# Attention and two expert layers in one kernel: own bank for the Sinkhorn sums, later conversions, token sums from turned tiles, work moved from VectorE to POOL

## The chip, the cores and the metric

The kernel runs on one core of a Trainium2 chip, as one launch. The metric is device time in microseconds, from a run without a profiler; a profiled execution is taken beside it. Five engines work at once, each through its own queue in order: TensorE (PE, with PEld for its weight loads), VectorE (DVE), ScalarE (ACT), GpSimd (POOL) and SyncE (SP), which issues all the transfers.

## The reference

Three blocks follow each other on 1536 tokens (two sequences of 768) with 512 features:

```python
# 1. banded attention, 8 heads of 64: key j is kept for query i where
#    0 <= i - j < 96, or j < 8; linear distance bias per head; softmax; times v
# 2. eight experts, all of them on every token, weighted by a Sinkhorn matrix
logits = x @ w_gate
P = np.exp(logits - logits.max())
for _ in range(8):
    P /= P.sum(1, keepdims=True) + 1e-09
    P /= P.sum(0, keepdims=True) + 1e-09
    P *= N / E
for e in range(E):
    out += P[:, e:e+1] * (np.maximum(x @ w1[e], 0.0) @ w2[e])      # 512 -> 1024 -> 512
# 3. h = max(x @ w1, x @ w2, x @ w3); result h @ w_out              # 512 -> 768 -> 512
```

All of it is in float32.

## The kernel before

Every float32 operand is split into an upper part, rounded for TensorE (`...h`, a ScalarE copy), and a lower part, the rest (`...l`, a subtraction on VectorE or POOL); a product is three matmuls, upper by upper, upper by lower and lower by upper.

**Attention** (`near_attention`, L415) runs over 48 units of 256 queries and one head, with one step per unit. In a step each engine gets work of three units: the scores of the next one, the turning and the value product of this and of the last one, and the splits of the one after. `s_min` and `s_norm` (L520, L546) are the softmax; `split_qk` and `split_v` (L450, L476) split queries, keys and values, the lower parts of keys and values on POOL; `x_evac` (L332) adds up two heads, writes x to DRAM (`xd`) and splits it. `tables_rest` (L141) makes the distance tables that units from number 8 on use. Expert 0's weights come in eight tiles `w0` at the steps of `W0AT` (2, 4, 6, 8 to 12): `w0_hi` (L193) copies the upper part, and `w0_lo` (L199) subtracts the lower part on VectorE, one step later. Expert 0 and the gate's logits run on TensorE between the units' matmuls.

**The expert loop** starts when attention ends. Experts 1 to 7 go through `w1` by a Strassen-like scheme: a group is 7 products of 2 by 3 matmuls instead of 8. A list of hooks, fillers and jobs, all with step numbers that are written out by hand, sets the order: group G starts at step 7G, and `REL` says at which step of a group each of its products stands (1:0, 2:2, 6:4, 7:8, 5:10, 4:12, 3:13, so that three groups overlap). A step holds a product, the hooks of that step, and one filler, which is mostly a piece of the output product. There are four passes: p = 0 and 1 are the experts for either half of the tokens (28 groups each), p = 2 and 3 are the third block (9 groups each, `base[2]` is step 392, `base[3]` 455). In p = 2 and 3, no output piece stands between the products for long stretches.

The products of a group write into PSUM banks `b1` (three buffers), `b2` (two) and `b3` (one); `BANK` assigns products 5 and 3 to `b2`, product 2 to `b3`. `keep` (L1162) copies a bank on ScalarE, `add` (L1197) adds another to it on VectorE, `fin` (L1177) applies the relu or the maximum and splits. Loads go through five buffers `raw` in the order of their job steps; `feed` (L938) issues as many as there are free buffers.

**Sinkhorn** (L886 to L926) runs beside the first 25 steps. A round is a row step on VectorE (`sink_rows`), a matmul with ones for the column sums (`col`) into bank `b3`, and the column step on VectorE (`turn`). **Conversions** (L1090) turn the third block's weights, which come as 64-bit numbers, into float32 on VectorE, nine passes each, 24 conversions from step 15 on, 14 steps apart; `sums_m` (L1008) then makes sums of weight blocks on POOL.

**Token sums.** The scheme needs four sums of x blocks, t1 to t4, for every pass. `chain_at` (L1058) loads two blocks from DRAM, subtracts on POOL (L1069), stores the result to `xt[p]` (L1070), and loads it again for the next of the four. For p = 2 and 3 x is the output of the experts: `x2_tile` (L1077) turns a tile of it on TensorE, ScalarE copies it, and it is stored to DRAM (`x2d`), from where `chain_at` reads. `put` (L1038) loads and splits the blocks and the sums.

Of the kernel before, what the change touches and what calls it, by code (L numbers as in the profile page):

```python
# [24 lines left out]
def kernel(  # L25
# [40 lines left out]
    def load_first(i, t):  # L66
# [74 lines left out]
    def tables_rest():  # L141
# [24 lines left out]
    xt = [dpool.tile([4, 128, 2 * QT], F32, name=f"xt{p}") for p in range(4)]  # L166
# [26 lines left out]
    def w0_hi(j):  # L193
        o = 0
        for (h, l), n in zip(w0[j], W0N[j]):
            nc.scalar.copy(h[:, 0:n], w0raw[j][:, o : o + n])
            o += n

# [133 lines left out]
    def x_evac(op, pool, o, hp, n):  # L332
# [8 lines left out]
        def late():  # L341
# [3 lines left out]
            nc.vector.tensor_tensor(  # L345
# [15 lines left out]
    def chain(p, raw, done, cols=slice(None)):  # L361


        def one(o, a, b, nm, free):
            def go():
                ro = raw(o)
                nc.gpsimd.tensor_tensor(out=ro, in0=raw(a), in1=raw(b), op=ALU.subtract)
                nc.sync.dma_start(out=xt[p][XT.index(nm)][:, cols], in_=ro)
                for f in free:
                    done(f)  # L370

            return go

        return [
            one("b11", "b12", "b11", "t1", ()), one("b12", "b22", "b12", "t3", ("b12",)),
            one("b22", "b22", "b11", "t2", ("b11",)),
            one("b21", "b21", "b22", "t4", ("b22", "b21")),
        ]

    def chain0():  # L380

        fs = []
        for kk in range(2):
# [6 lines left out]
            c = slice(kk * QT, kk * QT + QT)  # L390
            fs += [load, None] + chain(0, rr.get, lambda nm: None, c)
# [23 lines left out]
    def near_attention():  # L415
        with ExitStack() as st:
# [179 lines left out]
            def s_x(u):  # L596
# [4 lines left out]
                return x_evac(opu.pop(u // 2), ap, tb * 256, h // 2, 256)  # L601
# [11 lines left out]
            tables_rest()  # L613
# [5 lines left out]
            for s in range(NU + 1):  # L619
# [33 lines left out]
                if s in W0AT:  # L653
                    wlate = W0AT.index(s)
                    w0_hi(wlate)
# [21 lines left out]
    def full_attention():  # L677
        with ExitStack() as st:
# [4 lines left out]
            ps_y = st.enter_context(tc.tile_pool(name="gps_y", bufs=1, space=PSUM))  # L683
            for j in range(8):
# [169 lines left out]
    pools = {"b1": ps_b1, "b2": ps_b2, "b3": ps_b3, "yp": ps_y}  # L854
# [57 lines left out]
    def sink_turn(n):  # L912
        box = {}

        def col():
            box["ps"] = bank("b3", "c")
# [21 lines left out]
    def feed():  # L938
        while job_q and flying["n"] < 5 and job_q[0][3] <= flying["slot"]:
# [4 lines left out]
            elif k2 == "t":  # L944
                nc.sync.dma_start(out=r[:, 0 : 2 * QT], in_=src)
            elif k2 == "c":
                nc.sync.dma_start(out=r.bitcast(I32), in_=src)
            else:
# [65 lines left out]
    for u in range(9):  # L1014
        s = 28 * u + 50
# [30 lines left out]

    for p in range(4):
        for nm, r in USE.items():
            t = nm in XT
            src = xt[p][XT.index(nm)] if t else x_block(xd if p < 2 else x2d, p, nm)  # L1050
            job(base[p] - 6 + r, ("x", p, nm), src, "t" if t else "x", (-9, 177, base[1] + 185, base[2] + 48)[p])
# [4 lines left out]
    SUM = (("t1", "b12", "b11"), ("t3", "b22", "b12"), ("t2", "b22", "t1"), ("t4", "b21", "t2"))  # L1056

    def chain_at(p, s, d, src):  # L1058
        for n, (o, a, b) in enumerate(SUM):
            for x in (a, b):  # L1060
                t = x in XT
                job(
                    s + n * d, ("c", p, n, x), xt[p][XT.index(x)] if t else x_block(src, p, x),
                    "t" if t else "x", s + n * d - (d - 1 if t and d < 8 else 8),
                )

            def go(n=n, o=o, a=a, b=b):
# [369 lines left out]
```

## Time and profile before

| | |
|---|---|
| median of 3 runs | 1373.66 us (1373.36 to 1376.17) |
| profiled execution | 1376.38 us, its span 1374.6 us |
| instructions | 19793 |
| mean granted TensorE clock | 0.98 of full speed |
| busy in the span | PE 1319.0 us (96%), PEld 1190.9 (87%), DVE 948.5 (69%), ACT 700.8 (51%), POOL 645.9 (47%) |
| moved by DMA | 171.26 MB, 125 GB/s |

A busy share is the mean over stretches with different limits. Matmuls are pipelined, so the durations of single ones overlap; the distance from one to the next is what counts.

### The profile page before, as it was taken

The numbers are of one execution on the slowest core, as the hardware profiler recorded it, in microseconds if no ns is written. First come the engines' busy times: TensorE is split into PE (matmuls) and PEld (weight loads), VectorE is DVE, ScalarE is ACT, GpSimd is POOL, SyncE is SP. The second block draws the span as 40 slices with busy tenths as digits, with TensorE's granted clock in tenths as the row PEclk, the third lists the DMA queues.
The fourth block names the chain that finished last, engine by engine and source line by source line (L and its number), as shares of the span: only waits on it lengthen the run. The fifth ranks groups of instructions, "written<-read, shape, count | busy, mean of one in ns | idle before, by whom it ended". The sixth has DMA issues, their size and how long they took to land.

```text
span 1374.6 us, 19793 instructions
## 1 busy us (share of the span) xinstructions
PE 1319.0 (96%) x6984; PEld 1190.9 (87%) x6984; DVE 948.5 (69%) x1507; ACT 700.8 (51%) x1415; POOL 645.9 (47%) x716
## 2 busy tenths in 40 slices
PE   5899999879999999999999999999999999979998
PEld 3789998768888898889888888898898889878987
DVE  7877786586776878787888677677876556455361
ACT  6777776444444444454554454544444445445351
POOL 5545663236445555545455443454444442273251
PEclk8799999889999999999999999999999999999999
DMA  5543540432233343333454343432324135466231
GB/s 156 165 127 89 161 150 18 143 122 93 85 116 111 125 138 126 123 127 108 132 179 142 108 129 104 149 128 90 129 77 132 65 118 184 129 242 215 102 104 46
DMA packets 67307, 171.26 MB, mean 125 GB/s; under 512 B 6784, under 2 KB 25984, under 8 KB 67200
## 3 DMA queue, kind: packets, MB, share of 16 engines
q1 hardware_dynamic: 67200, 169.91, 38.4%
q8 instruction: 57, 0.93, 0.3%
q14 instruction: 50, 0.41, 0.1%
HBM read 143.15 MB, written 26.74 MB: 124 GB/s over the span
## 4 chain that ended last, share of the span: by engine, by line
PE 88%; DVE 5%; ACT 2%; issue 2%; DMA 1%; POOL 1%; DVEq 0%; SPq 0%; POOLq 0%; ACTq 0%
PE yp L238 42%; PE b L1156 35%; PE hp L221 5%; PE o L593 2%; PE t L567 2%; PE s L507 1%; DVE sal L961 1%; POOL raw L1069 0%; PE lp L298 0%; DMA x2d<-x2t 0%; DMA raw<-xt 0%; ACT sbh L979 0%; PE x L1081 0%; DVE u L1204 0%; DMA raw<-w 0%
## 5 line engine op out<-in xcount | busy, mean ns | idle before, releaser
L238 PE MATMUL yp<-w2h,xl 128*128 128x512 f32 x744 | 295.4, 397 | 0.0
L238 PE MATMUL yp<-w2l,xh 128*128 128x512 f32 x744 | 293.9, 395 | 0.0
L238 PE MATMUL yp<-w2h,xh 128*128 128x512 f32 x744 | 290.3, 390 | 0.0
L154 POOL TENSOR_TENSOR xl<-u,xh 128x384 fp32r<-128x384 f32 x112 | 115.8, 1034 | 349.7 <-ACT xh L153 345.3
L974 POOL TENSOR_TENSOR raw<-raw 128x256 f32<-128x256 f32 x260 | 230.7, 888 | 74.1 <-DVE sbl L961 49.0
L238 PEld LDWEIGHTS yp<-w2h,xl 128*128 128x128 f32 x744 | 139.6, 188 | 29.7
L238 PEld LDWEIGHTS yp<-w2h,xh 128*128 128x128 f32 x744 | 140.0, 188 | 18.8 <-DVE y L1254 0.5
L238 PEld LDWEIGHTS yp<-w2l,xh 128*128 128x128 f32 x744 | 139.6, 188 | 18.3
L1254 DVE SCALAR_TENSOR_TENSOR y<-yp,pm,y 128x512 f32<-128x512 f32 x168 | 124.3, 740 | 15.5 <-PE yp L238 15.4
L1164 ACT COPY u<-b 128x384 f32<-128x384 f32 x148 | 70.2, 477 | 119.0 <-PE b L1156 105.3
L1184 ACT ACTIVATE s<-s 128x384 f32<-128x384 f32 x56 | 29.5, 526 | 194.9 <-DVE s L1204 194.9
L961 DVE TENSOR_TENSOR sbl<-raw,sbh 128x768 fp32r<-128x768 f32 x56 | 75.2, 1342 | 62.9 <-ACT sbh L979 61.4
L226 DVE SCALAR_TENSOR_TENSOR xl<-b,xh 128x384 fp32r<-128x384 f32 x56 | 31.1, 555 | 106.0 <-ACT xh L225 104.8
L961 DVE TENSOR_TENSOR sal<-raw,sah 128x1024 fp32r<-128x1024 f32 x68 | 84.6, 1244 | 25.6 <-ACT sah L990 25.5
L1204 DVE TENSOR_TENSOR u<-b,u 128x384 f32<-128x384 f32 x136 | 74.6, 549 | 39.1 <-PE b L1156 37.8
L961 DVE TENSOR_TENSOR w2l<-raw,w2h 128x1024 fp32r<-128x1024 f32 x62 | 83.0, 1338 | 13.2 <-ACT w2h L1026 13.2
L1164 ACT COPY s<-b 128x384 f32<-128x384 f32 x74 | 35.4, 478 | 105.9 <-PE b L1156 105.8
L154 POOL TENSOR_TENSOR xl<-s,xh 128x384 fp32r<-128x384 f32 x56 | 59.7, 1066 | 53.6 <-ACT xh L153 53.6
L990 ACT CAST sah<-raw 128x1024 fp32r<-128x1024 f32 x74 | 77.3, 1044 | 4.5 <-POOL raw L974 2.5
L1184 ACT ACTIVATE u<-u 128x384 f32<-128x384 f32 x112 | 59.1, 528 | 24.0 <-DVE u L1204 24.0
L462 POOL TENSOR_TENSOR k<-kqv,k 128x384 fp32r<-128x384 f32 (+1 forms) x46 | 47.2, 1026 | 48.2 <-ACT k L461 48.2
L979 ACT CAST sbh<-raw 128x768 fp32r<-128x768 f32 x74 | 61.5, 832 | 10.5 <-DMA raw<-w 6.0
(275 smaller groups left out, 3573.9 us busy)
## 6 DMA issues: line engine op xcount, KB each, us to landing
raw<-w SPq DMA_DIRECT2D x163, 512.0 KB, 3.7
kqv<-a SPq DMA_DIRECT2D x32, 416.0 KB, 3.2
raw<-w32s SPq DMA_DIRECT2D x18, 512.0 KB, 4.1
raw<-xt SPq DMA_DIRECT2D x22, 384.0 KB, 3.2
raw<-x2d SPq DMA_DIRECT2D x18, 384.0 KB, 3.9
w<-cb SPq DMA_DIRECT2D x24, 256.0 KB, 2.3
raw<-xd SPq DMA_DIRECT2D x12, 384.0 KB, 4.1
w32s<-raw SPq DMA_DIRECT2D x9, 512.0 KB, 2.6
```

The lines of the kernel that those rows point to most:

```text
L154: lo_eng.tensor_tensor(out=lo, in0=src, in1=hi.bitcast(F32), op=ALU.subtract)
L221: nc.tensor.matmul(ps, a[:, q], b, start=k == 0, stop=k == 11)
L238: nc.tensor.matmul(ps, a, b, start=kf == first and i == 0, stop=kf == last and i == 2)
L961: (eng or nc.vector).tensor_tensor(out=l, in0=src, in1=h.bitcast(F32), op=ALU.subtract)
L974: nc.gpsimd.tensor_tensor(out=b[o], in0=b[x], in1=b[z], op=op)
L979: nc.scalar.copy(h, r)
L990: nc.scalar.copy(h, jobs[key])
L1156: nc.tensor.matmul(s[BANK[m]], a[:, c], b[:, kk], start=k == 0 and m in FIRST, stop=k == 5 and m in LAST, skip_group_check=True,)
L1164: nc.scalar.copy(t, st[G]["b1"])
L1184: nc.scalar.activation(src, src, AF.Relu)
L1204: nc.vector.tensor_tensor(out=o, in0=s[b], in1=s[nm], op=ALU.add)
L1254: nc.vector.scalar_tensor_tensor(out=y[n], in0=ps, scalar=pm[:, n, e : e + 1], in1=y[n], op0=ALU.mult, op1=ALU.add)
```

## The change

- Attention: the gate's weights are made (POOL) at the end of step 0 instead of ahead of the loop; `tables_rest` moves from ahead of the loop to step 1, and its six copies from VectorE to POOL. The lower parts of the first four `w0` tiles are subtracted on POOL in parts of 256 columns, two per step, instead of on VectorE in one go. For the first 256 tokens, `x_evac`'s lower part is on POOL.
- PSUM: `b2` has one buffer instead of two; a new bank `c` takes the column sums of Sinkhorn and the turned tiles. The Sinkhorn start stands ahead of the first `s_sum`, and the rounds are at steps 2, 5, ... 23 instead of 1, 4, 7, 10, 13, 17, 20, 24.
- Conversions, `sums_m` and the token sums of pass 1 start 14 steps later.
- `xt[p]` is stored as eight blocks of 384 columns instead of four of 768. For p = 2 and 3 the sums are taken on POOL from two turned tiles in SBUF, 256 columns each, and stored once per pair.
- The output product of pass 2 (`o_piece`) is divided by features: twelve matmuls of the first two feature blocks per tile from step `base[3]` - 6 on, copied out by ScalarE, and six of the last block after `base[3]` + 8, added by VectorE; before it was nine and nine in one PSUM bank after `base[3]` + 8.

```diff
-    nc.gpsimd.memset(wg2.bitcast(F32)[:, :, 2 * E :], 0.0)
-    nc.gpsimd.tensor_copy(wg2[:, :, 0:E], wgr)
-    nc.gpsimd.tensor_tensor(
-        out=wg2[:, :, E : 2 * E], in0=wgr, in1=wg2[:, :, 0:E].bitcast(F32), op=ALU.subtract
-    )
+    def gate_weights():
+        nc.gpsimd.memset(wg2.bitcast(F32)[:, :, 2 * E :], 0.0)
...
-            nc.vector.tensor_copy(dst, src)
+            nc.gpsimd.tensor_copy(dst, src)
...
-    xt = [dpool.tile([4, 128, 2 * QT], F32, name=f"xt{p}") for p in range(4)]
+    xt = [dpool.tile([8, 128, QT], F32, name=f"xt{p}") for p in range(4)]
...
+    def w0_lo_parts(j):
+        def one(h, l, n, o, last):
+            def go():
+                c = slice(n, n + 256)
+                nc.gpsimd.tensor_tensor(
+                    out=l[:, c], in0=w0raw[j][:, o : o + 256], in1=h.bitcast(F32)[:, c],
+                    op=ALU.subtract,
+                )
...
-            nc.vector.tensor_tensor(
+            eng.tensor_tensor(
                 out=xvl[:, o // 256, hp, c], in0=tmp, in1=hi.bitcast(F32), op=ALU.subtract
             )
...
+                eng = nc.gpsimd if tb == 0 else nc.vector
...
-            tables_rest()
+            wparts = []
...
                 if s in W0AT:
-                    wlate = W0AT.index(s)
-                    w0_hi(wlate)
+                    j = W0AT.index(s)
+                    w0_hi(j)
+                    if j < 4:
+                        wparts += w0_lo_parts(j)
+                    else:
+                        wlate = j
+                for f in wparts[:2]:
+                    if f():
+                        consumed()
+                wparts = wparts[2:]
+                if s == 0:
+                    gate_weights()
+                if s == 1:
+                    tables_rest()
...
-    ps_b2 = ctx.enter_context(tc.tile_pool(name="ps_b2", bufs=2, space=PSUM))
+    ps_b2 = ctx.enter_context(tc.tile_pool(name="ps_b2", bufs=1, space=PSUM))
+    ps_c = ctx.enter_context(tc.tile_pool(name="ps_c", bufs=1, space=PSUM))
...
-            box["ps"] = bank("b3", "c")
+            box["ps"] = bank("c", "c")
...
-        s = 28 * u + 50
+        s = 28 * u + 64
...
+    C1 = {o: 106 + 28 * n for n, (o, _, _) in enumerate(SUM)}
+    P2 = [base[1] + 50 + 28 * i for i in range(3)]
+    P3 = [base[2] + 21 + 4 * i for i in range(3)]
...
+            ready = (-9, C1[nm] + 1 if t else -9, P2[2] + 6, P3[2] + 6)[p]
...
+    def x2_sums(p, i):
+        t = i if p == 2 else 6 + i
+        a, b = x2t.pop(t), x2t.pop(t + 3)
+        r = jobs["x2", p, i]
+        t1, t2, t3, t4 = [r[:, 256 * n : 256 * n + 256] for n in range(4)]
+        lo, hi = slice(0, 256), slice(256, 512)
+        for o, x, z in (
+            (t1, b[:, lo], a[:, lo]), (t2, b[:, hi], t1), (t3, b[:, hi], b[:, lo]),
+            (t4, a[:, hi], t2),
+        ):
+            nc.gpsimd.tensor_tensor(out=o, in0=x, in1=z, op=ALU.subtract)
+        nc.sync.dma_start(
+            out=xt[p][:, :, 128 * i : 128 * (i + 1)].rearrange("a p n -> p a n"),
+            in_=r.rearrange("p (a n) -> p a n", a=8),
+        )
+        done(("x2", p, i))
+
+    for p, ss, d in ((2, P2, 2), (3, P3, 1)):
+        for i, s in enumerate(ss):
+            t = i if p == 2 else 6 + i
+            job(s + d, ("x2", p, i), None, None, s - 8)
+            at(s, lambda t=t: x2_tile(t))
+            at(s + d, lambda t=t: x2_tile(t + 3))
+            at(s + 2 * d, lambda p=p, i=i: x2_sums(p, i))
...
-    for t in range(6):
-        fillers.append((base[2] + 20 + t, lambda s, t=t: x2_tile(6 + t, "yp")))
-    for t in range(6):
-        fillers.append((base[3] + 8, o_piece(2, t, (0, 3, 1), True, False)))
-        fillers.append((base[3] + 8, o_piece(2, t, (4, 2, 5), False, True)))
+    for i, t in [(i, t) for i in range(2) for t in range(6)]:
+        s = base[3] + (8 + t if i else 2 * t - 6)
+        fillers.append((s, o_piece(2, t, ((0, 3, 1, 4), (2, 5))[i], i == 0, i == 1, True)))
...
-        convert(n // 2, n % 2, 14 * n + 15)
-    chain_at(1, 92, 28, xd)
-    for t in range(6):
-        at(base[1] + 43 + 7 * t, lambda t=t: x2_tile(t, "b2"))
-    chain_at(2, 288, 28, x2d)
-    chain_at(3, base[2] + 36, 4, x2d)
-
-    for n, c in enumerate((1, 4, 7, 10, 13, 17, 20, 24)):
+        convert(n // 2, n % 2, 14 * n + 29)
+
+    for n, c in enumerate(range(2, 24, 3)):
...
-        2: (lambda: s_sum(0), sink_start, lambda: s_add(1)),
+        2: (sink_start, lambda: s_sum(0), lambda: s_add(1)),
```

## Rows read from the trace of the kernel before

**Rows 1.** Busy time by stretch: PE, PEld, DVE, ACT, POOL, clock, DMA share, GB/s.
```profile
12.00:56.00 44.00, 34.14 (x148) 27.05 (x149) 36.71 (x107) 33.08 (x100) 23.97 (x42) 0.69 0.52 151
...
256.00:311.00 55.00, 41.60 (x194) 37.15 (x194) 41.94 (x96) 25.89 (x45) 20.18 (x23) 0.86 0.35 113
311.00:1184.00 873.00, 873.00 (x4355) 783.65 (x4355) 627.45 (x775) 420.73 (x729) 423.17 (x429) 1.00 0.37 120
1184.00:1257.00 73.00, 62.49 (x346) 59.10 (x345) 42.19 (x53) 33.38 (x59) 36.94 (x22) 0.95 0.64 211
```

**Rows 2.** Chain that ended last, attention stretch: start us, us, what.
```profile
12.61 1.13 DVE db L150 x3
...
23.89 1.64 DVE w_0l L202
...
40.61 1.91 DVE w_2l L202
```

**Rows 3.** Timeline of POOL and DVE in attention: start us, us, instruction.
```profile
8.24 0.50 POOL L486 TENSOR_TENSOR vhl<-y,vhl 128x128 fp32r<-128x128 f32 x1
...
19.32 0.74 POOL L462 TENSOR_TENSOR k<-kqv,k 128x256 fp32r<-128x256 f32 x1
...
42.45 0.15 DVE L550 TENSOR_SCALAR am<-am 128x2 f32<-128x2 f32 x1
...
44.47 1.19 POOL L462 TENSOR_TENSOR k<-kqv,k 128x384 fp32r<-128x384 f32 x1
...
44.83 0.86 DVE L550 TENSOR_SCALAR am<-am 128x2 f32<-128x2 f32 x1
```

**Rows 4.** Chain that ended last, expert loop.
```profile
262.42 2.29 PE b L1156 x6
...
310.60 0.23 PE c L917 x2
310.83 2.16 PE yp L238 x6
...
1184.44 2.09 PE b L1156 x12
1186.52 0.44 PE x L1081 x4
...
1192.11 6.35 DMA x2d<-x2t
...
1228.57 3.87 DMA raw<-w
...
1349.14 21.82 PE yp L238 x96
```

**Rows 5.** Timeline of DVE at the start of the expert loop.
```profile
254.28 0.68 DVE L226 SCALAR_TENSOR_TENSOR xl<-hp,xh 128x512 fp32r<-128x512 f32 x1
...
262.20 0.17 DVE L920 TENSOR_SCALAR cs<-c 128x8 f32<-128x8 f32 x1
...
263.98 0.33 DVE L893 TENSOR_REDUCE cs<-pm 128x8 f32<-128x96 f32 x1
```

**Rows 6.** The page's costliest groups, whole span: busy, mean ns | idle before, releaser.
```profile
L974 POOL TENSOR_TENSOR raw<-raw 128x256 f32<-128x256 f32 x260 | 230.7, 888 | 74.1 <-DVE sbl L961 49.0
...
L961 DVE TENSOR_TENSOR sal<-raw,sah 128x1024 fp32r<-128x1024 f32 x68 | 84.6, 1244 | 25.6 <-ACT sah L990 25.5
...
L979 ACT CAST sbh<-raw 128x768 fp32r<-128x768 f32 x74 | 61.5, 832 | 10.5 <-DMA raw<-w 6.0
```

**Rows 7.** Timeline of PE and DVE after 1184: product 5 and the add.
```profile
1216.18 0.54 DVE L1204 TENSOR_TENSOR u<-b,u 128x384 f32<-128x384 f32 x1
...
1217.13 0.33 PE L1156 MATMUL b<-t1h,sah 128*128 128x384 f32 x1
...
1225.52 0.33 PE L1156 MATMUL b<-t1h,sah 128*128 128x384 f32 x1
...
1227.80 0.54 DVE L1204 TENSOR_TENSOR u<-b,u 128x384 f32<-128x384 f32 x1
```

More of the change, by code (lines that the diff above doesn't have):

```diff
@@ L104 @@
     lg = const.tile([128, NTT, E], F32, name="lg")
-    nc.gpsimd.memset(wg2.bitcast(F32)[:, :, 2 * E :], 0.0)
-    nc.gpsimd.tensor_copy(wg2[:, :, 0:E], wgr)
-    nc.gpsimd.tensor_tensor(
-        out=wg2[:, :, E : 2 * E], in0=wgr, in1=wg2[:, :, 0:E].bitcast(F32), op=ALU.subtract
-    )
+    def gate_weights():
+        nc.gpsimd.memset(wg2.bitcast(F32)[:, :, 2 * E :], 0.0)
+        nc.gpsimd.tensor_copy(wg2[:, :, 0:E], wgr)
+        nc.gpsimd.tensor_tensor(
+            out=wg2[:, :, E : 2 * E], in0=wgr, in1=wg2[:, :, 0:E].bitcast(F32), op=ALU.subtract
+        )
     nc.vector.tensor_copy(rel[:, 0], ri)
@@ L197, in w0_hi @@
             o += n
+    def w0_lo_parts(j):
+        def one(h, l, n, o, last):
+            def go():
+                c = slice(n, n + 256)
+                nc.gpsimd.tensor_tensor(
+                    out=l[:, c], in0=w0raw[j][:, o : o + 256], in1=h.bitcast(F32)[:, c],
+                    op=ALU.subtract,
+                )
+                if last:
+                    w0raw.pop(j)
+                return last
+            return go
+        fs, o = [], 0
+        for (h, l), m in zip(w0[j], W0N[j]):
+            for n in range(0, m, 256):
+                fs.append(one(h, l, n, o, o == 768))
+                o += 256
+        return fs
     def w0_lo(j):
@@ L359, in x_block, with t_block @@
         return src[k : k + 2, :, n : n + QT].rearrange("k p n -> p k n")
[L361 to L378, printed above, removed]
+    def t_block(p, nm):
+        i = 2 * XT.index(nm)
+        return xt[p][i : i + 2].rearrange("k p n -> p k n")
     def chain0():
@@ L388, in load, with one, go @@
                     nc.sync.dma_start(out=rr[nm], in_=xd[k + kk, :, n : n + QT])
-            c = slice(kk * QT, kk * QT + QT)
-            fs += [load, None] + chain(0, rr.get, lambda nm: None, c)
+            def one(o, a, b, nm, kk=kk, rr=rr):
+                def go():
+                    nc.gpsimd.tensor_tensor(out=rr[o], in0=rr[a], in1=rr[b], op=ALU.subtract)
+                    nc.sync.dma_start(out=xt[0][2 * XT.index(nm) + kk], in_=rr[o])
+                return go
+            fs += [
+                load, None, one("b11", "b12", "b11", "t1"), one("b12", "b22", "b12", "t3"),
+                one("b22", "b22", "b11", "t2"), one("b21", "b21", "b22", "t4"),
+            ]
         return fs
@@ L1049, with go, x2_tile @@
             t = nm in XT
-            src = xt[p][XT.index(nm)] if t else x_block(xd if p < 2 else x2d, p, nm)
-            job(base[p] - 6 + r, ("x", p, nm), src, "t" if t else "x", (-9, 177, base[1] + 185, base[2] + 48)[p])
+            src = t_block(p, nm) if t else x_block(xd if p < 2 else x2d, p, nm)
+            ready = (-9, C1[nm] + 1 if t else -9, P2[2] + 6, P3[2] + 6)[p]
+            job(base[p] - 6 + r, ("x", p, nm), src, "x", ready)
             if base[p] - 6 + r >= 0:
                 at(base[p] - 6 + r, lambda p=p, nm=nm: put(p, nm))
-    SUM = (("t1", "b12", "b11"), ("t3", "b22", "b12"), ("t2", "b22", "t1"), ("t4", "b21", "t2"))
-    def chain_at(p, s, d, src):
-        for n, (o, a, b) in enumerate(SUM):
-            for x in (a, b):
[L1061 to L1067, printed above, removed]
-                ra, rb = [jobs["c", p, n, x][:, 0 : 2 * QT] for x in (a, b)]
-                nc.gpsimd.tensor_tensor(out=ra, in0=ra, in1=rb, op=ALU.subtract)
-                nc.sync.dma_start(out=xt[p][XT.index(o)], in_=ra)
-                for x in (a, b):
-                    done(("c", p, n, x))
-            at(s + n * d, go)
-    def x2_tile(t, tag):
-        ps = bank(tag, "x2")
+    for n, (o, a, b) in enumerate(SUM):
+        for x in (a, b):
+            t = x in XT
+            job(
+                C1[o], ("c", n, x), t_block(1, x) if t else x_block(xd, 1, x), "x",
+                C1[x] + 1 if t else -9,
+            )
+        def go(n=n, o=o, a=a, b=b):
+            ra, rb = [jobs["c", n, x][:, 0 : 2 * QT] for x in (a, b)]
+            nc.gpsimd.tensor_tensor(out=ra, in0=ra, in1=rb, op=ALU.subtract)
+            nc.sync.dma_start(
+                out=t_block(1, o), in_=ra.rearrange("p (k n) -> p k n", k=2)
+            )
+            for x in (a, b):
+                done(("c", n, x))
+        at(C1[o], go)
+    x2t = {}
+    def x2_tile(t):
+        ps = bank("c", "x2")
         p4 = ps.rearrange("p (k n) -> p k n", k=4)
```

44 lines of the change are left out of this document (27 added, 17 removed).

## The prediction, made before the changed kernel was run

> **What bounds the kernel now.** I read three views. The busy time by stretch comes first [rows 1]: from 311 to 1184 us TensorE is busy for all 873 us at full clock, so nothing that the change does there can gain, it can only cost. What can be gained lies in three places: the attention stretch 12 to 56 (TensorE 34.1 of 44 us, granted clock 0.69 as a mean of the two levels, VectorE 36.7, POOL 24.0), the start of the expert loop 256 to 311 (TensorE 41.6 of 55, VectorE 41.9), and 1184 to 1257 (62.5 of 73). Second, the chain that ended last, in order of time, says what TensorE waits for there. In the attention stretch it runs through VectorE: the last three of the six table copies, then a lower part of expert 0's weights every second step [rows 2]. After 256 a product at 262.42 takes 2.29 us where one takes 1.04, and the first expert output piece comes as late as 310.83 [rows 4]. After 1184 it holds two transfers, 6.35 and 3.87 us [rows 4]. Third, single instructions, for prices [rows 3, 5, 6, 7].
>
> Units: a product (six matmuls of 384) is 1.04 us, half of the 2.09 for twelve; an output matmul of 512 is 0.227 (21.82 for 96), so an output piece of six is 1.36 [rows 4].
>
> **Part 1, attention (steps 0 to 9).** VectorE loses four lower parts (1.64 to 1.91, at 1.8 that is 7.1 us), six copies (1.13 for three, so 2.3), and four x lower parts (a quarter of 1.64 each, 1.6): 36.7 becomes 25.7. POOL gains 16 quarter parts. One with 256 columns takes it 0.74 us alone [rows 3], and 0.89 as a mean where others run [rows 6], so 11.8 to 14.2; four x lower parts, 3.0 to 3.6; six copies, no such POOL row exists: between nothing and 0.50 each, the price of the 128-column subtract [rows 3], I take 0.3, so 1.8; and the three gate instructions, moved in from before 12 us, about 1.0 by the same row. That is 17.6 to some 21: POOL goes from 24.0 to 41.6 to 45 of 44 us. So the bound moves from VectorE to POOL and the stretch keeps its length. In order: a step's last two parts stand ahead of the next step's key split, for which the scores wait, and of the scaling, for which the turns wait; the earlier reciprocal is then waited out on POOL. The ends: if POOL keeps up, what stood on the chain is gone, minus 8 (7.1 and 1.1); if POOL gets in VectorE's way, plus 7 (next sentences). I take 0, nearest to the row with POOL at 24.0 before the additions.
>
> That they get in each other's way is a row: VectorE's two-column add takes 0.15 at 42.45, and 0.86 at 44.83, where it ends with POOL's key split, 44.47 plus 1.19 [rows 3]. Ten steps with 0.7 each, on the path to the scaling, are the plus 7. The Trainium skill says it as a rule (SBUF — State Buffer, Who interferes with whom): VectorE and GpSimd share a pair of ports under an exclusive lock held for the whole instruction, and the one that comes second blocks fully. The trace agrees (0.86 for 0.15). By that rule the part that moves work to POOL would cost; it is rival C below.
>
> **Part 2, start of the expert loop (steps 0 to 24).** Now: product 2 shares its bank with the Sinkhorn column sum, so TensorE waits until VectorE has read that sum, and VectorE gets there late, behind lower parts and the first conversion. Three edits act together: a bank of its own for the sum; the Sinkhorn start ahead of the first lower part in VectorE's order, with rounds every 3 steps; conversions 14 steps later. TensorE's work until the first output piece: 21 products (21.9), 8 pieces (10.9), 8 sums of 0.23 [rows 4] (1.8), together 34.6 us; it took 54.8 (256 to 310.83). What is late next is VectorE, since the sums still wait for its rounds. Its work up to the last sum: start 2.4, seven rounds of 2.1 (262.20 to 263.98 and 0.33 [rows 5]), four 1024-column lower parts of 1.24 [rows 6], seven of 768 at 0.93 by their columns, nine adds and splits of 0.55 [rows 7], two output weight parts of 1.24: 2.4 + 14.7 + 5.0 + 6.5 + 5.0 + 2.5 = 36.1. It is free for this at 255.0 [rows 5], so 291 at the earliest. I add 5: about 2.4 for one lower part that waits for four ScalarE passes of up to 0.83 [rows 6] behind a product, the rest for blocking by POOL. Last sum 296, then a product: first output piece at 297.3 in place of 310.83, minus 13.5. That piece also ran in part at the lower clock after the wait (2.16 for 1.36), 0.8 more: minus 14. Ends: minus 20 with TensorE alone (34.6), minus 6 if only the conversion's passes go and the order still stalls.
>
> The conversions themselves cost nothing later: they fall into steps where TensorE is full and VectorE has 627 of 873 us [rows 1]; if that cover went, a conversion is some 6 us. The token sums for pass 1 and 2 lie under the same cover, and so do the smaller runs of the `xt` loads, which have five buffers to run ahead.
>
> **Part 3, the last products (from 1184).** From the first product after the last output piece (1184.44) to TensorE's end (1349.14 and 21.82 [rows 4]) are 186.5 us. The work in it: 111 products (116.0), six turned tiles of 0.44 [rows 4] (2.6), 216 output matmuls (49.1): 167.7. Lost: 19. Today x goes out to DRAM, back, through four dependent subtractions with a store and a load between each, and SP, one queue in order, holds the weight loads behind these stores: the 6.35 and 3.87. After the change the four subtractions read the turned tiles in SBUF, and the blocks are ready 13 steps earlier; that takes away about 12 of the 19. Six output parts of 2.7 (twelve matmuls) also move among the steps in which pass 3's blocks are split, which gives VectorE and ScalarE time there; the six extra adds on VectorE lie beside TensorE.
>
> What is late next. POOL: 12 subtractions of 0.89 are 10.7 us [rows 6] within ten steps (some 12 us), beside the lower parts that it has there already: one of these comes up to 2 us late. ScalarE: three buffers hold the turned tiles until POOL has read them, up to 1. And the bank: product 5 of the next group now waits for the add that reads product 3's sum, which had a second bank. In the present trace the add ends at 1216.72 with the next product 5 at 1217.13, but at 1228.34 where that product 5 started at 1225.52 [rows 7]: it would have held TensorE 2.8. The late one hangs on a late load that goes, so I put 0 to 0.5 on each of 12 groups, 3 in all. Gain 12 minus 3: minus 9. Ends: 0 and minus 13.
>
> **Sum.** 0, minus 14, minus 9: minus 23. The profiled execution took 1376.4 us with a span of 1374.6, 2.7 over the median of the runs. 1376.4 minus 23 is 1353.4; carried to the median, 1350.7: **1351 us**.
>
> **Rivals.**
> A. Attention gains after all: POOL had 20 us of slack, VectorE led the chain. Against: POOL's sum of 41.6 and more. Front minus 8: 1343. Chance 0.13.
> B. The late stretch doesn't gain: the wait moves from the DRAM chain to POOL's 10.7 us and SP's three stores behind them. For: POOL's load; against: nothing dependent lies between the subtractions. 1351 + 9 = 1360. Chance 0.12.
> C. POOL and VectorE block each other in attention, plus 7: 1358. With it go the cases where the expert loop gains only its lower end, plus 8: 1359. Chance 0.17.
> D. Slower: the single second bank turns the steps without output pieces into a loop through VectorE. There are 17 groups from 1184 on, and in two of three VectorE has a 1024-column lower part ahead of the add. With the 2.8 of rows 7 in 12 groups that is 34 us, less the 23: 1385. It decides from a mean lateness of 1.9 (23 over 12). Against it: 1216.72 before 1217.13. In the full stretch it can't happen, a step there is 2.4 us and the add has four of them. Chance 0.06.
> E. The change does next to nothing, because the sums still wait for VectorE as long as now and the gains cancel: 1374. Chance 0.04.
>
> The forecast itself has 0.48, and for itself 1346 to 1356. The range takes in A, B and C, which are all on the same side, as well as most of the ends of the parts: 1341 to 1364. About 0.2% (2.7 us) is what a measurement of this kernel tells from no change. Faster by more: forecast, A, B and C, 0.90. Within: E, 0.04. Slower: D, 0.06.
>
> **What would show it.** In the changed profile: the first output piece near 297 (part 2), and no product there released by the read of a column sum; POOL near full from 12 to 56 and the scaling released by POOL's own queue instead of the reciprocal (part 1); no store and load of token sums on the chain after 1184, and what TensorE loses there near 10 of the present 19 (part 3). A product 5 released by VectorE's add group after group would be D. The forecast is wrong if TensorE's loss in the attention stretch changes by more than 5, or if the expert loop's start gains less than 10.

## The result and the profile after

The changed kernel takes 1359.32 us (median of 4 runs, 1358.68 to 1361.51); the kernel before took 1374.91 beside it (1373.36 to 1376.37). The ratio is 0.9887, 95% interval 0.9875 to 0.9899: faster by 1.1%. The forecast was 1351 with a range of 1341 to 1364, so the time lies in the range, 8 us above the forecast. The profiled execution took 1361.51 us, its span 1359.7, that is 14.9 less than the span before.

First the busy time by stretch, the columns as in [rows 1]:

```profile
12.00:56.00 44.00, 34.74 (x160) 30.00 (x161) 30.15 (x95) 35.30 (x106) 40.77 (x72) 0.69 0.53 157
256.00:311.00 55.00, 48.38 (x233) 43.61 (x232) 41.51 (x89) 29.21 (x50) 23.66 (x27) 0.91 0.30 94
1176.00:1248.00 72.00, 69.40 (x381) 64.83 (x380) 38.89 (x51) 35.13 (x61) 35.49 (x29) 1.00 0.58 178
```

Against [rows 1], POOL in the attention stretch went from 23.97 to 40.77 and VectorE from 36.71 to 30.15, but TensorE's busy time in it hardly changed (34.14 to 34.74). At the loop's start TensorE is busy for 48.4 of 55 us instead of 41.6, and after the last expert output piece (now at 1175.70) for 69.4 of 72 instead of 62.5 of 73.

The chain that ended last, whose rows of before are [rows 2, 4] (start us, us, what):

```profile
26.47 1.56 POOL w_0l L207 x2
28.02 0.69 POOL k L482
...
43.13 1.56 POOL w_2l L207 x2
...
274.50 1.07 DVE pm L957
...
275.88 0.96 DVE rs L923
...
281.68 1.14 DVE sbl L994
...
297.73 0.59 PE c L952 x2
298.33 2.12 PE b L1222 x6
300.45 2.56 PE yp L263 x6
303.00 1.20 PE b L1222 x6
...
1175.70 3.14 PE b L1222 x18
...
1262.08 2.71 PE yp L263 x6
1264.78 1.56 PE b L1222 x6
```

In attention, POOL's quarter parts and the key split behind them stand where VectorE's lower parts stood. At the loop's start the first output piece comes at 300.45 instead of 310.83; the last column sum stands just ahead of it at 297.73, and the product and the piece behind it take 2.12 and 2.56 where 1.04 and 1.36 are usual. No transfer stands in the chain after 1175.70 any more.

What TensorE still waits for, its timeline (start us, us, instruction, in brackets the idle time before it and what ended it):

```profile
285.77 0.39 PE L952 MATMUL c<-cs,ones 128*128 128x8 f32 x2 [2.37 <-DVE cs L928]
297.73 0.59 PE L952 MATMUL c<-cs,ones 128*128 128x8 f32 x2 [3.44 <-DVE cs L928]
...
716.27 0.50 PE L263 MATMUL yp<-w2h,xh 128*128 128x512 f32 x1 [1.07 <-DVE y L1320]
...
1187.42 0.66 PE L1122 MATMUL x<-ident,y 128*128 128x128 f32 x4 [1.54 <-ACT x2t L1124]
...
1262.08 0.57 PE L263 MATMUL yp<-w2h,xh 128*128 128x512 f32 x1 [3.00 <-DVE osb L1366]
...
1302.52 0.44 PE L1222 MATMUL b<-b22h,sah 128*128 128x384 f32 x1 [1.67 <-DVE u L1270]
...
1308.19 0.44 PE L1222 MATMUL b<-t1h,sah 128*128 128x384 f32 x1 [1.20 <-DVE u L1270]
```

Product 2 waits for nothing at the start; the column sums' own matmuls do. New are the wait at 716 (the third block's weight sums now meet a change of pass), those on the turned tiles (three, 2.4 us together) and on the output pieces' adds (3.00), and one wait of product 5 on its single bank (1.20). The wait of 1302.52 was there before.

Why the add at 1262 was late stands in VectorE's timeline:

```profile
1258.77 2.19 DVE L994 TENSOR_TENSOR b22l<-raw,b22h 128x768 fp32r<-128x768 f32 x1 [2.05 <-ACT b22h L1075]
1260.88 0.55 DVE L1270 TENSOR_TENSOR s<-b,s 128x384 f32<-128x384 f32 x1
1261.35 0.67 DVE L1366 TENSOR_TENSOR osb<-yp,osb 128x512 f32<-128x512 f32 x1
```

The first add stands behind b22's lower part, which waits for its ScalarE copy and then takes 2.19 where the one before it at 1255.31 took 0.95.

Four stages by their first and last matmuls, in us, tell where a kernel's time goes: up to the last logits' matmul of attention; from there to the first matmul of the first expert output piece (loop start); to the last of the last piece (steady); and to the end (late).

| kernel | attention | loop start | steady | late | ratio to before, 95% interval |
|---|---|---|---|---|---|
| before | 238.8 | 71.9 | 873.4 | 186.5 | |
| changed | 237.3 | 62.9 | 875.1 | 180.5 | 0.9887 (0.9875 to 0.9899) |
| 1 attention back | 237.3 | 60.8 | 874.8 | 180.6 | 0.9893 (0.9878 to 0.9907) |
| 2 banks back | 236.5 | 65.8 | 874.9 | 180.3 | 0.9904 (0.9889 to 0.9918) |
| 3 conversions back | 236.0 | 67.3 | 875.6 | 180.6 | 0.9920 (0.9907 to 0.9933) |
| 4 output pieces back | 237.2 | 61.5 | 875.2 | 180.3 | 0.9872 (0.9855 to 0.9889) |
| 5 Sinkhorn order back | 236.5 | 65.1 | 876.5 | 179.2 | 0.9900 (0.9886 to 0.9913) |
| 6 chain through DRAM back | 236.9 | 62.5 | 875.1 | 189.5 | 0.9952 (0.9939 to 0.9965) |
| 7 no POOL sums at the start | 236.7 | 60.8 | 874.0 | 181.7 | 0.9877 (0.9862 to 0.9893) |
| 8 second parts later | 236.1 | 61.5 | 874.9 | 178.0 | 0.9864 (0.9849 to 0.9880) |
| 9 chain and pieces back | 237.0 | 62.1 | 875.3 | 187.9 | 0.9938 (0.9926 to 0.9950) |
| 10 spread | 237.2 | 61.5 | 877.8 | 177.6 | 0.9882 (0.9866 to 0.9897) |
| 11 spread, POOL relieved | 237.3 | 62.4 | 876.3 | 176.6 | 0.9859 (0.9844 to 0.9875) |
| 12 first output weights on POOL | 237.2 | 63.1 | 875.9 | 174.2 | 0.9866 (0.9851 to 0.9882) |

The eight kernels whose loop start is the changed one's (changed, 1, 4, 6, 8 to 11) show 60.8 to 62.9 for it, 61.9 in the mean: so 1 us in a stage of one profile is not a difference, and the gain there is 10, of which the profiled execution shows 9. Between two ratios 0.001 is 1.4 us, less than their intervals' half width (1.7 to 2.3); smaller steps are read from the stages. What TensorE *loses* at a place is, in the following, by how much its matmuls there stand further apart than without a wait at full clock.

### The profile page after: what moved, and what is told of

It reads as the page before. It is cut to its first block, busy times and chain, and to the rows that moved or that the text cites. A ratio compares the mean times of both kernels' runs of the same rounds, so it can differ in the third digit from the quotient of the medians.

```text
span 1359.7 us, 19797 instructions
## 1 busy us (share of the span) xinstructions
PE 1315.0 (97%) x6984; PEld 1191.0 (88%) x6984; DVE 942.9 (69%) x1498; ACT 702.4 (52%) x1415; POOL 661.6 (49%) x758
## 4 chain that ended last, share of the span: by engine, by line
PE 89%; DVE 5%; POOL 2%; issue 2%; ACT 2%; DVEq 0%; POOLq 0%; ACTq 0%
PE yp L263 42%; PE b L1222 37%; PE hp L246 5%; PE o L613 2%; PE s L527 2%; PE t L587 2%; DVE sal L994 1%; PE lp L323 0%; PE x L1122 0%; DVE w2l L994 0%; POOL nn L573 0%; ACT sbh L1012 0%; DVE pm L957 0%; POOL k L482 0%; POOL raw L1007 0%
## 5 line engine op out<-in xcount | busy, mean ns | idle before, releaser
L994 DVE TENSOR_TENSOR sbl<-raw,sbh 128x768 fp32r<-128x768 f32 x56 | 68.7, 1226 | 61.8 <-ACT sbh L1012 61.8
L994 DVE TENSOR_TENSOR sal<-raw,sah 128x1024 fp32r<-128x1024 f32 x68 | 84.2, 1238 | 21.8 <-ACT sah L1023 21.7
L994 DVE TENSOR_TENSOR w2l<-raw,w2h 128x1024 fp32r<-128x1024 f32 x62 | 83.1, 1341 | 12.6 <-ACT w2h L1059 12.6
L1059 ACT CAST w2h<-raw 128x1024 fp32r<-128x1024 f32 x62 | 65.2, 1051 | 0.1
```

The lines of the kernel that those rows point to most:

```text
L994: (eng or nc.vector).tensor_tensor(out=l, in0=src, in1=h.bitcast(F32), op=ALU.subtract)
L1059: nc.scalar.copy(h, r)
```

## The experiments

The first four each take one part of the change back.

**1. Attention back.** Gate weights ahead of the loop, and:

```diff
-            nc.gpsimd.tensor_copy(dst, src)
+            nc.vector.tensor_copy(dst, src)
-                    if j < 4:
-                        wparts += w0_lo_parts(j)
-                    else:
-                        wlate = j
+                    wlate = j
-                eng = nc.gpsimd if tb == 0 else nc.vector
+                eng = nc.vector
```

> The changed kernel with the attention part undone: gate weights before the loop, the six table copies, the lower parts of expert 0's first four weight parts and the x lower parts of the first token block on VectorE again. My theory: the attention stretch only swapped its bound (VectorE for POOL), worth 1 to 1.5 us by the markers; so 1360.5, plus 1 against the changed kernel, and the first product of the last expert 0 part near 243. Rival (POOL carries it with slack, and the later stretches hide a gain of 8): plus 5 to 8, 1365 to 1367. Rival (POOL's load costs): minus 3 or more.

Measured 1360.95, 0.8 above the changed kernel by the ratios, within their intervals; the attention stage is 237.3 in both. VectorE has 38.2 of the 44 us again and POOL 25.6. So the stretch only swapped its bound, as the theory had it; both rivals fall.

**2. Banks back.**

```diff
-    ps_b2 = ctx.enter_context(tc.tile_pool(name="ps_b2", bufs=1, space=PSUM))
-    ps_c = ctx.enter_context(tc.tile_pool(name="ps_c", bufs=1, space=PSUM))
+    ps_b2 = ctx.enter_context(tc.tile_pool(name="ps_b2", bufs=2, space=PSUM))
-            box["ps"] = bank("c", "c")
+            box["ps"] = bank("b3", "c")
-        ps = bank("c", "x2")
+        ps = bank("b2" if t < 6 else "yp", "x2")
```

> The changed kernel with the banks of before: the column sum shares product 2's bank again, no fourth pool, two buffers for product 5's bank, turned tiles of pass 2 in product 5's bank and of pass 3 in the output bank; order of the rounds, conversions and token sums as changed. My theory: VectorE's rounds set the loop's start and the own bank gives product 2 what it waited for, about half of the gain there; without it the first output piece comes 3 to 6 us later (303 to 306), while the waits on the turned tiles' single bank (2.4) and on product 5's single bank (1.2) after 1170 go: net 0 to plus 3, 1359 to 1362. Rival (the own bank is all of the gain at the start): plus 9 or more there, the first output piece near 310. Rival (rounds alone bind): the first output piece stays at 300 to 301 and the whole is 3 to 4 us faster, 1355.5.

Measured 1363.24, plus 2.3; loop start plus 3.9, late the same. TensorE's timeline of this kernel:

```profile
295.99 0.45 PE L1221 MATMUL b<-b21h,sbh 128*128 128x384 f32 x1 [2.69 <-DVE cs L954]
...
1198.70 0.44 PE L1221 MATMUL b<-b11h,sbl 128*128 128x384 f32 x1 [1.41 <-POOL sbl L993]
...
1204.74 0.44 PE L1221 MATMUL b<-t2h,sal 128*128 128x384 f32 x1 [1.58 <-POOL sal L993]
```

At the start product 2 waits for the read of a column sum again (2.69): the own bank is worth 4 of the 10. In the late stage the expected 3.6 didn't come: the turned tiles no longer wait, but POOL's lower parts do instead, 1.41 and 1.58 later. So the tiles' single bank alone is not what costs there; 11 below comes back to it.

**3. Conversions back.**

```diff
-        convert(n // 2, n % 2, 14 * n + 29)
+        convert(n // 2, n % 2, 14 * n + 15)
```

> The changed kernel with the conversions of the float64 weights 14 steps earlier, as before (first one at step 15). My theory: the first conversion's eight passes (some 6 us of VectorE) fall among the last Sinkhorn rounds again and push the last column sum and the first output piece back by 3 to 6.5: 1362.5 to 1366. Rival (VectorE waits for ScalarE and product banks there, so passes fit beside): 0, 1359. A gain of about 1 elsewhere is possible, as the stall near 714 us may go.

Measured 1365.30, plus 4.5; loop start plus 5.4 against the mean of the unchanged ones. VectorE's timeline ahead of the last round, and the sum that waits for it:

```profile
295.92 0.69 DVE L1189 SCALAR_TENSOR_TENSOR cb<-raw,cs 128x512 int32<-128x512 int32 x1
296.64 1.37 DVE L1192 TENSOR_TENSOR cb<-cb,cs 128x512 f32<-128x512 f32 x1
298.04 0.69 DVE L1193 SCALAR_TENSOR_TENSOR cb<-cb,ct 128x512 f32<-128x512 f32 x1
```

```profile
300.80 0.38 PE L952 MATMUL c<-cs,ones 128*128 128x8 f32 x1 [7.42 <-DVE cs L928]
```

The wait before the last sum grows from 3.44 to 7.42. VectorE's work is what the loop's start waits for.

**4. Output pieces back.** Nine and nine matmuls in one bank from step 8 of pass 3 on, copied out by ScalarE:

```diff
-    for i, t in [(i, t) for i in range(2) for t in range(6)]:
-        s = base[3] + (8 + t if i else 2 * t - 6)
-        fillers.append((s, o_piece(2, t, ((0, 3, 1, 4), (2, 5))[i], i == 0, i == 1, True)))
+    for t in range(6):
+        fillers.append((base[3] + 8, o_piece(2, t, (0, 3, 1), True, False)))
+        fillers.append((base[3] + 8, o_piece(2, t, (4, 2, 5), False, True)))
```

> The changed kernel with pass 2's output pieces as before: one bank for all 18 matmuls of a token tile, from step 8 of pass 3 on, evicted by ScalarE, no add on VectorE. My theory: the waits for VectorE's adds near 1262 (3.0 us and some 2 at the lower clock behind them) go, but the splits of pass 3's blocks again fall into steps with products alone and cost 2 to 4 there: net minus 3 to 0, 1356 to 1359. Rival (the early parts are worth more than the adds cost): plus 2 or more.

Measured 1359.30; 2.1 less by the ratios, whose intervals overlap, and the late stage is the same within 0.2. Without the early pieces to spread them, products that wait for VectorE take the adds' place:

```profile
1232.47 0.44 PE L1222 MATMUL b<-t1h,sah 128*128 128x384 f32 x1 [1.84 <-DVE u L1270]
```

With the lower clock behind it TensorE loses 3.6 there, for the 4.9 at 1262. The theory holds at its zero end.

The next four take the other parts of the change and two suspected costs.

**5. Sinkhorn order back**, with the own bank and the late conversions kept:

```diff
-        2: (sink_start, lambda: s_sum(0), lambda: s_add(1)),
+        2: (lambda: s_sum(0), sink_start, lambda: s_add(1)),
-    for n, c in enumerate(range(2, 24, 3)):
+    for n, c in enumerate((1, 4, 7, 10, 13, 17, 20, 24)):
```

> The changed kernel with the Sinkhorn order of before: its start behind the first group's lower part on VectorE, column sums at steps 1, 4, 7, 10, 13, 17, 20, 24; own bank, late conversions and all else as changed. My theory: of the 9 to 10 us at the loop's start the late conversions have some 4.5 and the own bank some 3, so the order has 1 to 3 left: the first output piece at 300 to 303, the whole plus 1 to 2. Rival (VectorE's work up to the last sum is the same in any order, so order is worth nothing): 0. Rival (the last sum at step 24 instead of 23 stands behind more lower parts): plus 4 or more.

Measured 1362.39, plus 1.8; loop start plus 3.2. The first sum already waits:

```profile
260.35 0.38 PE L952 MATMUL c<-cs,ones 128*128 128x8 f32 x1 [3.05 <-DVE cs L928]
```

So of the 10 us at the start, taking back the bank, the conversions or the order costs 3.9, 5.4 or 3.2, together 12.5. That is more than the 10, so what one of them saves may hang in part on the others; but 2.5 over three profiles is near the scatter.

**6. Chain through DRAM back** for passes 2 and 3, with its `chain_at(2, 288, 28, x2d)` and `chain_at(3, base[2] + 36, 4, x2d)` in place of `x2_sums`.

> The changed kernel with the token sums of passes 2 and 3 through DRAM as before: turned tiles stored, two blocks loaded, one subtraction on POOL, stored and loaded again for the next; xt in eight blocks, all else as changed. My theory: the chain cost some 8 of the 19 us lost after 1184 before, and what the late stretch gave back came from the output pieces' adds and the single bank of product 5, which are still in: plus 5 to 8, with a wait of TensorE of 4 to 5 for a load again. Rival (the gain of 6 there came from taking pass 2's output pieces early, and POOL's subtractions now cost what the chain cost): 0 to plus 2.

Measured 1369.33, plus 8.9, all of it in the late stage (189.5 for 180.5). Its timeline of TensorE:

```profile
1218.05 0.69 PE L1221 MATMUL b<-t1h,sah 128*128 128x384 f32 x1 [3.19 <-DVE u L1269]
...
1223.87 0.69 PE L1221 MATMUL b<-t4h,sbh 128*128 128x384 f32 x1 [1.61 <-ACT u L1229]
```

and ScalarE's, which shows what the two waits stand behind:

```profile
1214.81 1.05 ACT L1023 CAST sah<-raw 128x1024 fp32r<-128x1024 f32 x1 [2.53 <-DMA raw<-w32s]
...
1222.61 0.83 ACT L1012 CAST sbh<-raw 128x768 fp32r<-128x768 f32 x1 [3.26 <-DMA raw<-w]
```

Two weight loads are late, as before [rows 4]: VectorE's add stands behind the lower part of the first, ScalarE's copy of `u` behind the second. The waits are 4.8 together, the lower clock behind them takes 4.0 more. The sum is just beyond the upper end of what was expected. Since 189.5 is 3.0 above the 186.5 of before, the rest of the late edits cost 3.

**7. No POOL sums at the start.** The weight sums of the first five groups are left out, so their products use unsummed weights:

```diff
     def s_add(G):
-        sum_up(jobs["s", G])
+        if G > 4:
+            sum_up(jobs["s", G])
```

> The changed kernel without the four POOL additions each that make the weight sums of the first five groups (their products then use unsummed weights, so the output is not the reference's); all instructions of the other engines stay. Theory (POOL holds VectorE's short operations at the loop's start): the Sinkhorn passes that took 0.8 to 1.06 take 0.17 to 0.27 again, the sum of what was stretched, 2 to 4 us, goes from the last column sum and the first output piece. Rival (VectorE's waits for ScalarE and for the column sums themselves set the end): 0 to minus 1.

Measured 1358.96, 1.4 less, within the intervals; loop start 60.8, 1.1 below the mean of the unchanged ones. VectorE's timeline and the last sum:

```profile
274.27 0.34 DVE L957 SCALAR_TENSOR_TENSOR pm<-pm,cs 128x96 f32<-128x96 f32 x1
...
275.40 0.97 DVE L925 TENSOR_TENSOR pm<-pm,rs 128x96 f32<-128x96 f32 x1
```

```profile
295.03 0.38 PE L952 MATMUL c<-cs,ones 128*128 128x8 f32 x1 [3.85 <-DVE cs L928]
```

Line 957 took 1.07 in this round with the sums and 0.34 without, so POOL's work does hold VectorE's short operations. But line 925 now meets a POOL lower part (0.97 for 0.26), and the last sum waits as long as before. Nearer to the rival: POOL's sums cost about 1 us there, not 2 to 4.

**8. Second parts later.**

```diff
-        s = base[3] + (8 + t if i else 2 * t - 6)
+        s = base[3] + (10 + t if i else 2 * t - 6)
```

> The changed kernel with the second parts of pass 2's output pieces (six matmuls and VectorE's add) two steps later, from step 10 of pass 3 instead of step 8. My theory: the third of them waits 3.0 us because VectorE's first add stands behind a lower part that waits for ScalarE and for POOL (b22's, 2.19 us); two steps of products (2.1 us) in between cover most of it, and the lower clock behind the wait goes too: minus 2 to minus 4 (of the 4.9 lost near 1262), 1355 to 1357. Rival (products in these two steps wait for the same lower part and for product 5's single bank instead): 0.

Measured 1356.64, 3.2 less by the ratios, and 2.5 in the late stage. The wait on the add is still there, shorter, with no lower clock behind it:

```profile
1260.37 0.50 PE L263 MATMUL yp<-w2h,xh 128*128 128x512 f32 x1 [1.36 <-DVE osb L1366]
```

So the adds did cost, and it was their place in VectorE's queue, not their number.

The last four: what gave back the 3 us, and whether the waits go when the work is spread.

**9. Chain and pieces back**, the edits of 6 and 4 together.

> The changed kernel with both the token sums of passes 2 and 3 through DRAM and pass 2's output pieces as before; of the late edits only the single bank of product 5 is left, so from the last expert output piece to the end it differs from the kernel before by that. That stretch was 186.5 us before, 180.5 in the changed kernel, 189.5 with the chain alone back. Theory that the divided pieces cost the 3 which the late stretch gave back: 186.5, that is plus 6 on the whole. Theory that product 5's single bank costs them: 189 to 190, plus 9.

Measured 1367.64, plus 7.0, late stage 187.9: between the two theories. Product 5's bank shows itself in

```profile
1240.50 0.44 PE L1221 MATMUL b<-t1h,sah 128*128 128x384 f32 x1 [1.84 <-DVE u L1269]
```

By the stages the single bank costs 1.4 (187.9 for 186.5) and the divided pieces 1.6 (189.5 for 187.9), both near the scatter of a stage: how the 3 divide stays open. `xt` in eight blocks is still in this kernel too, and no run takes it back by itself.

**10. Spread.**

```diff
-        s = 28 * u + 64
+        s = 28 * u + 60
-            s[BANK[m]] = bank(BANK[m], BANK[m])[:, 0:QT]
+            tag = "c" if m == 5 and groups[G][0] == 3 and G % 2 else BANK[m]
+            s[BANK[m]] = bank(tag, BANK[m])[:, 0:QT]
-        s = base[3] + (8 + t if i else 2 * t - 6)
+        s = base[3] + (11 + t if i else 2 * t - 6)
-        (base[3] + 35, 3, 0), (base[3] + 37, 3, 1), (base[3] + 39, 3, 2),
+        (base[3] + 22, 3, 0), (base[3] + 29, 3, 1), (base[3] + 36, 3, 2),
```

> The changed kernel with the second output parts of pass 2 from step 11 of pass 3, the third block's weight sums at steps 28u+60 instead of 28u+64, the last output weights' splits at steps 22, 29 and 36 of pass 3 (where VectorE has no other work in its order) instead of 35, 37, 39, and product 5 of every second group of pass 3 in the bank that the turned tiles have left. My theory: the losses near 1262 (4.9 with the clock), 715 (1.35) and 1302 to 1308 (3.4) are all VectorE or POOL work bunched in one step, so spreading it takes most of them: minus 6 to minus 9, 1350 to 1353. Rival (VectorE's load, and the lower parts that POOL stretches, only move the waits to other steps): minus 3, as for the output parts alone.

Measured 1359.88, 0.7 less: a miss for the theory. Two of the edits only moved the waits, as TensorE's timeline shows:

```profile
715.98 0.50 PE L263 MATMUL yp<-w2h,xh 128*128 128x512 f32 x1 [3.07 <-DVE y L1321]
...
1294.57 0.44 PE L1223 MATMUL b<-b22h,sah 128*128 128x384 f32 x1 [2.46 <-DVE cm L1271]
```

With the weight sums four steps earlier the wait near 716 is longer (3.07 for 1.07; with the clock behind it 4.9 are lost), and at 1294 a split of the output weights stands ahead of the add that product 3 waits for. The output pieces' and product 5's waits are gone. The late stage is 2.9 shorter, the steady one 2.7 longer.

**11. Spread, POOL relieved.** On top of 10:

```diff
-        ps = bank("c", "x2")
+        ps = bank("yp" if t >= 9 else "c", "x2")
-        lower(h, l, r, nc.gpsimd if groups[G][0] >= 2 else nc.vector)
+        lower(h, l, r, nc.gpsimd if p == 3 or p == 2 and i not in (4, 5, 6) else nc.vector)
```

and the lower part of group 5's summed weights in pass 2 on VectorE too.

> The kernel with the work spread and, on top, pass 3's second set of turned tiles in an output bank, and four lower parts of the three groups beside them on VectorE instead of POOL. My theory: TensorE's waits on the turned tiles' bank (3.2 us from 1179 to 1194) and, behind them, on POOL's lower parts (0.5; 3.5 when only the bank was changed back) come from POOL's subtractions, so with both gone minus 2.5 to minus 3.5 against the spread one. Rival (VectorE's lower parts there come late in their turn, as with the bank alone): 0.

Measured 1357.09, 3.2 less than 10 by the ratios. Between 1176 and 1206 TensorE loses 0.6, where it lost 3.7 in the changed kernel and 3.5 with the banks alone (2): so POOL's load and the bank had to go together. POOL's load alone wasn't taken away.

**12. First output weights on POOL.** On top of 11:

```diff
-            lower(h, l, r)
+            lower(h, l, r, nc.gpsimd if key == 0 else nc.vector)
```

> The one before with, on top, the lower parts of the first expert's first two output weight tiles (steps 18 and 20) on POOL instead of VectorE. Theory that VectorE's work up to the last column sum sets the first output piece: 2.4 us of work and 1.4 of waiting for ScalarE leave VectorE ahead of the last round, the first output piece 2 to 3.5 earlier, and as much on the whole. Rival (POOL's two lower parts of 2.4 us stretch VectorE's short operations by as much, or hold POOL's other lower parts there): 0 to plus 1.

Measured 1356.99, the same as 11 within the intervals; loop start 63.1 for 62.4. The rival holds. VectorE's timeline, and POOL's beside it:

```profile
291.40 2.23 DVE L994 TENSOR_TENSOR sal<-raw,sah 128x1024 fp32r<-128x1024 f32 x1 [0.38 <-ACT sah L1024]
...
294.45 1.52 DVE L957 SCALAR_TENSOR_TENSOR pm<-pm,cs 128x96 f32<-128x96 f32 x1
```

```profile
290.14 5.71 POOL L994 TENSOR_TENSOR w2l<-raw,w2h 128x1024 fp32r<-128x1024 f32 x2
```

POOL's two lower parts take 5.71, and beside them VectorE's takes 2.23 instead of 1.22, and line 957 takes 1.52 where it takes 0.81 in the last round of the changed kernel and 0.26 undisturbed. The work that left VectorE came back as longer instructions. The Trainium skill (SBUF — State Buffer, Who interferes with whom) says that the two engines share a pair of ports under an exclusive lock; this trace agrees, with 2.23 for 1.22.

Kernels 8, 11 and 12 are the fastest: 1.3 to 1.4% below the kernel before, 3 to 4 us below the changed one, at the edge of what the intervals part. The version that they point to, 12 with the weight sums left at 28u+64, wasn't run.

## Why the prediction was right, and where it wasn't

**Part 1, attention: 0, measured 0 against kernel 1.** POOL came to 40.77 of 44 us, 41.6 were worked out, and the chain runs through it. VectorE kept 30.15 where 25.7 was worked out. The scaling on POOL, which waited three times for the reciprocal in this stretch (1.53 to 1.55 us each), now does so once (0.40), as was forecast. Kernel 1 shows the stage at the same length, 237.3, with either bound.

**Part 2, loop start: minus 14, measured minus 9 in the profile and 10 in the mean.** The mechanism was right: each of the three edits has its part (3.2, 3.9 and 5.4 when taken back), no product is released by the read of a column sum, and VectorE's work sets the last sum. The step that failed is "Last sum 296, then a product: first output piece at 297.3", with "0.8 more" for the clock. The last sum came at 297.73 (295.85 to 297.26 in the other kernels with this start), 1.7 late. VectorE waited 4.7 for ScalarE ahead of it, in three places (1.43, 1.87 and 1.38), where one wait of 2.4 was put. And TensorE had waited 3.44 for it, and behind the wait sum, product and piece took 0.59, 2.12 and 2.56, 5.3 in place of 2.6 (0.23, 1.04 and 1.36): 2.6 us of lower clock. The piece ended at 303.0 in place of 298.7, and these two are the 4.3 between. The prediction gave the lower clock back with the wait, though by its own sum TensorE, with 34.6 us of work, still had to wait for VectorE. All the other kernels bear this out: behind the wait for the last sum each loses 1.6 to 3.1 us, and the loss is as large after a wait of 2.37 (kernel 5: 3.1) as after one of 7.42 (kernel 3: 3.1). The prediction's own sign of being wrong, a start that gains less than 10, lies just on the measured 9 to 10.

**The steady stretch: 0, measured plus 1.7.** "They fall into steps where TensorE is full" was said of the conversions. Kernel 3, which has them 14 steps earlier, keeps the wait near 716 (1.07, at 719.85 there), so they don't cause it. What the prediction left out is that the weight sums move by 14 steps too: eight POOL sums in a row now run at the change of pass, beside two of VectorE's splits. Timeline of POOL and DVE, changed kernel:

```profile
711.68 7.96 POOL L1007 TENSOR_TENSOR raw<-raw 128x256 f32<-128x256 f32 x8 [0.69 <-DVE cb L1192]
712.19 1.49 DVE L994 TENSOR_TENSOR sbl<-raw,sbh 128x768 fp32r<-128x768 f32 x1
713.60 1.49 DVE L994 TENSOR_TENSOR b22l<-raw,b22h 128x768 fp32r<-128x768 f32 x1
```

and the first of the same two splits in the kernel before, where POOL is idle at its start (the second takes 0.95 as well):

```profile
722.04 0.95 DVE L961 TENSOR_TENSOR sbl<-raw,sbh 128x768 fp32r<-128x768 f32 x1
```

Each now takes 0.54 longer, which together is the wait of 1.07, and TensorE loses 1.35 there. The mean busy time of VectorE over 873 us, on which the prediction rested, can't show one such place.

**Part 3, late: minus 9, measured minus 6.0.** Place by place, in us that TensorE loses:

| | before | changed |
|---|---|---|
| the chain's stretch, 1184 to 1238 before, 1175 to 1230 now | 12.5 | 3.7 |
| where pass 3's blocks are split, 1253; now the output pieces, 1262 | 2.0 | 4.9 |
| product 3 at 1317; now 1302 | 1.9 | 1.9 |
| other groups of pass 3 | 1.7 | 1.5 |

"That takes away about 12 of the 19" fits the first line, 12.5. What stays there is 3.7: POOL's late lower part 0.5, where up to 2 was named, and the turned tiles 3.2, where up to 1 was; kernel 11 takes both away. But the 3 of "Gain 12 minus 3" stood for something else, product 5's single bank ("0 to 0.5 on each of 12 groups"), and that costs one wait of 1.20 in this stage (one of 1.84 besides in kernels 4 and 9, without the early pieces). So it is luck that 12 minus 3 agrees with 12.5 minus 3.7. The step that failed is "the six extra adds on VectorE lie beside TensorE": at 1262 TensorE waits 3.00 and runs 1.9 behind at the lower clock, and the net of that line is plus 2.9, the 3 that are missing. Kernel 8 gets 2.5 of them back with two steps of distance. In the whole late stage of the changed kernel TensorE loses 12.0 by the table, where near 10 was forecast.

**The rivals.** A falls with kernel 1, and so does the part of C that lies in attention. B falls by the 6.0 and by kernel 6. D needed a lateness of 1.9 in each of 12 groups; one wait of 1.20 is there. E falls. The time is that of rival C's second half, 1359, but not by its cause alone: of the 8 us above the forecast 5 are Part 2's, 3 Part 3's and 1.7 the steady stretch's, less 1.5 in attention, which kernel 1, with the old attention at 237.3, doesn't bear out.

## What to carry to other kernels

When a wait is only made shorter, count the lower clock behind it as still there: here it went on to cost 1.6 to 3.1 us behind waits of 2.37 to 7.42, and was gone behind one of 1.36 (kernel 8) and, in one of two kernels, behind one of 2.46 (below). An addition moved to an engine with much idle time costs nothing only if no instruction ahead of it in that queue waits for a third engine; the busy share doesn't tell, the timeline at that step does. And work that moved from VectorE to POOL gained nothing in either place where both were the bound: in attention the stage kept its length (kernel 1), and at the loop's start POOL's long subtractions came back as longer instructions on VectorE (kernel 12).

## What the runs showed of the hardware

**The clock behind a wait.** The same code with the same wait of TensorE went on at different clocks. Timeline of TensorE and window (columns as in [rows 1]) of kernel 11:

```profile
1290.74 0.69 PE L1224 MATMUL b<-b22h,sah 128*128 128x384 f32 x1 [2.46 <-DVE cm L1272]
```

```profile
1290.00:1300.00 10.00, 9.26 (x39) 9.26 (x40) 4.92 (x7) 2.64 (x4) 4.03 (x2) 0.68 0.52 171
```

And the same of kernel 12, which differs from it only at the loop's start:

```profile
1290.93 0.44 PE L1224 MATMUL b<-b22h,sah 128*128 128x384 f32 x1 [2.46 <-DVE cm L1272]
```

```profile
1290.00:1300.00 10.00, 9.03 (x50) 8.71 (x51) 7.24 (x10) 3.57 (x7) 4.66 (x3) 1.00 0.70 219
```

At 0.68, a mean of the levels 1.2 and 2.4 GHz, 39 matmuls fit where 50 do at full clock; kernel 11 lost 5.3 us there and kernel 12 2.7. That is the whole difference between their late stages (176.6 and 174.2). Which of the two a wait of 2 to 3 us brings, these runs don't settle. At the loop's start it is the same: of the eight kernels with the changed start, four (1, 4, 8, 10) lose 1.7 us behind the last sum's wait and take 60.8 to 61.5 for the stage, the other four lose 2.6 to 2.9 and take 62.1 to 62.9.

**A clock that didn't matter.** Over the attention stretch the granted clock was 0.69 in the changed kernel and 1.00 in kernel 4, whose attention is the same:

```profile
12.00:56.00 44.00, 34.83 (x163) 29.19 (x163) 30.66 (x97) 36.16 (x109) 40.87 (x72) 1.00 0.51 153
```

The stage took 237.3 and 237.2. Of the twelve kernels with this attention, the four with 0.69 took 237.2 to 237.3, the four with 0.73 236.0 to 237.0, and the four with 1.00 236.5 to 237.2. So where TensorE waits for POOL and VectorE, the lower clock costs half a us in the mean at 0.69 and nothing at 0.73.
